# Padding a four-row broadcast matmul to 128 rows inside a fused attention and feed-forward kernel

## The chip, the cores and the metric

The kernel runs on one core of a Trainium2 chip. The metric is the device time of one execution in microseconds (us). Three runs of the kernel before gave 1332.72, 1333.96 and 1334.77 us, so the median is 1333.96 us. Engines are named TensorE (PE; PEld is its weight load), VectorE (DVE), ScalarE (ACT), GpSimd (POOL) and SyncE (SP, which here only issues DMAs).

## The reference

Three layers follow one another on a batch of 8 with 576 tokens: a linear attention with 8 heads of 64, a gated feed-forward (512 to 1024 and back), and a second one with a convolution over tokens.

```python
def phi(x):
    proj = np.einsum('bhsd,df->bhsf', x, w_phi)
    proj = proj - np.max(np.abs(proj), axis=-1, keepdims=True)
    return np.concatenate([np.exp(proj), np.exp(-proj)], axis=-1)
q_p, k_p = phi(q), phi(k)
kv = np.einsum('bhsf,bhsd->bhfd', k_p, v)
z = np.sum(k_p, axis=2)
num = np.einsum('bhsf,bhfd->bhsd', q_p, kv)
den = np.einsum('bhsf,bhf->bhs', q_p, z)[..., None] + 1e-06
x = num / den                                   # heads side by side: 512 wide
# first feed-forward: token shift, k = relu(xk @ w_k), v = k*k @ w_v
x = sigmoid(xr @ w_r) * v
# second: h = relu(x @ w_in), c = convolution of h over 3 tokens
out = (h * sigmoid(c)) @ w_out
```

## The kernel before

Heads go in pairs: 8 batches of 4 pairs, 32 pairs in all, and a pair makes one 128-row chunk of the transposed input of the first feed-forward. Attention of one pair runs beside the projections of the next one (function `attention`), and from pair 5 on the first feed-forward runs between attention's steps, a share at a time (`moe`). When attention ends, at about 830 us, the rest of the first feed-forward follows, then the second one. Most products are made of three products of halves in float32r ("hi" and "lo", `mm3`, L143 to L145).

The names in the trace: `ps` are projections (L247 to L251), `pkv` the products of keys and values (L304), `pt` transposes (L333), `pn` numerators with the denominator as 65th row (L359); `psk`, `psr`, `psv` belong to the first feed-forward, `psh` and `pso` to the second.

The division works like this. The two heads' denominators go by DMA into a tile `den` of 96 partitions; VectorE takes the reciprocal and splits it in hi and lo (`r4`); four DMAs on SyncE's queue (L386) lay these out as four rows of `rr`: two heads, hi and lo, 576 tokens each. Then the function `last` spreads each head's row over that head's 64 partitions with a matmul (L398): the stationary operand `on2` has 4 rows of ones and zeros and 128 columns, the moving one is `rr`, 4 rows and 288 columns, one half of the tokens at a time. The result `pr` is multiplied with the numerators into `xt` (L401), the chunk of the feed-forward's input. `last` is called a pair later, so that the DMAs have time.

There are 64 such matmuls, two for each pair. The order of the work is set by a scheduler that goes by its own costs, with attention's steps at higher priority than the feed-forward's; the two matmuls of a pair end up side by side or with other products between them.

```python
on2 = const.tile([4, P], F32R, name="on2")
V.tensor_copy(on2, on0)
...
rr = pool.tile([4, S], F32R, tag="rr", bufs=1, name="rr")
for i in range(4):
    SY.dma_start(f(rr[i:i + 1]), f(r4[:, i // 2, i % 2]))
...
T.matmul(pr, on2, rr[:, hf * HS:hf * HS + HS], start=True, stop=True)
```

Of the kernel before, what the change touches and what calls it, by code (L numbers as in the profile page):

```python
# [9 lines left out]
F32R = mybir.dt.float32r  # L10
# [5 lines left out]
P = 128  # L16
B, H, S, D = 8, 8, 576, 64
NP = H // 2          # head pairs; a pair is one 128-row chunk of d_model
DM, DFF, FT = 512, 1024, 128
KC = DM // P         # 4  # L20
FC = DFF // P        # 8
TMPS = 4             # tiles for what is soon used up
XT = 6               # chunks of x^T on chip
PSM = 3              # PSUM banks of the feed-forward while attention runs
# pairs from the first on whose projections and numerators take float32 products,
# while the tensor engine has time, and whose projections lie in the feed-forward's banks
NAT, NATN, PP = 6, 8, 5
# the feed-forward runs from the attention of pair MS on, slower up to pair SLOW
MS, SLOW, SR = 5, 9, 7.5
# steps of attention(pair) after which a part of the first feed-forward's weights is split  # L30
WAT = {p: (0, 8) for p in range(4)} | {-1: (0,), 4: (0, 4, 8, 12), 5: range(0, 17, 3), 6: range(17), 7: range(17)}
NB = 12              # the first of these parts, of 512 columns; the others have 256
DS0 = 10             # the second feed-forward's weights are split from this pair's attention on
HS = S // 2          # 288 tokens: one PSUM bank holds a half of a batch's tokens
V1 = D + 1
# columns of a head pair: q's tokens in order, k's last 64 tokens, k's first 512 tokens.
# Their nine tiles of 128 go by banks; the one in the middle holds the last 64 of q and of k.
W = 2 * S
BANKS = [(5, 6), (7, 8), (4,), (0, 1), (2, 3)]
DP = 6               # a head's 576 denominators as 96 partitions of 6  # L40


@with_exitstack
def fused_kernel(ctx: ExitStack, tc: tile.TileContext, qk, va, wphi, ones2, mu, wk, wv, wr, win, wout, cw, out):
# [9 lines left out]
    def f(x):  # L54
        return x.bitcast(F32)

    def from_f64(raw, h, c):
        """float32 of float64 given as their words, into c; h is room: cut to 24 bits,
        kept within float32's range, and zero below its normal numbers."""
        high, low = raw[:, :, 1], raw[:, :, 0]  # L60
        hu, cu = h.bitcast(U32), c.bitcast(U32)
        # the high word read as a float32 rises with the magnitude: 0x47efffff is that of the
        # largest float32; the squares of those of 2^-127 and 2^-126 lie around the threshold
        G.tensor_scalar(h, f(high), -122879.9921875, 122879.9921875, ALU.max, ALU.min)
        V.tensor_scalar(cu, hu, 3, 0x3FFFFFF8, ALU.logical_shift_left, ALU.bitwise_and)
        V.scalar_tensor_tensor(cu, hu, 0xC0000000, cu, ALU.bitwise_and, ALU.bitwise_or)
        V.scalar_tensor_tensor(cu, low, 29, cu, ALU.logical_shift_right, ALU.bitwise_or)
        A.activation(h, h, AF.Square)
        V.scalar_tensor_tensor(c, h, 2.0 ** -30 * 1.125, c, ALU.is_ge, ALU.mult)
# [14 lines left out]

# [1 line left out]
    ident = const.tile([P, P], F32, name="ident")  # L86
# [11 lines left out]
    V.tensor_tensor(wpl, wp0, f(wph), ALU.subtract)  # L98
    on2 = const.tile([4, P], F32R, name="on2")
    V.tensor_copy(on2, on0)  # L100
    mu1 = const.tile([P, 2, KC], F32, name="mu1")
    V.tensor_scalar(mu1, mu0, -1.0, 1.0, ALU.mult, ALU.add)
# [1 line left out]
    def weight(n, name):  # L104
        """Room for a weight [128, n], split."""
        hi = wpool.tile([P, 4096], F32R, tag="w", name=name + "h")
        lo = wpool.tile([P, 4096], F32R, tag="w", name=name + "l") if n == 4096 else None
        return hi[:, :n], lo[:, :n] if lo is not None else hi[:, n:2 * n]

    def weight_dram(src, name):  # L110
        """As above, into DRAM, by and by."""
        d = [dram.tile([P, 4096], F32, name=name + x) for x in "hl"]
        steps = []
        for o in range(0, 4096, 256):
            def load(o=o):
                raw = main.tile([P, 256, 2], U32, tag="raww", bufs=1, name="raww")
                SY.dma_start(raw, src[:, o:o + 256])
                return raw

            def step(raw, o=o):  # L120
                hc = tmps.tile([P, 2, 256], F32, tag="tmp", name="hc")
                from_f64(raw, hc[:, 0], hc[:, 1])
                w = tmps.tile([P, 2, 256], F32R, tag="tmp", name="whl")
                A.copy(w[:, 0], hc[:, 1])
                V.tensor_tensor(w[:, 1], hc[:, 1], f(w[:, 0]), ALU.subtract)
                for i in range(2):
                    SY.dma_start(d[i][:, o:o + 256], f(w[:, i]))
            steps.append((load, step))
        return d, steps
# [18 lines left out]

    # =============== attention and the first feed-forward ===============
    with ExitStack() as p1:  # L150
# [7 lines left out]
        def raw_room(n):  # L158
            # room that the feed-forward and the later pairs have no need of yet
            if n > 256:  # L160
                nraw[0] += 1
                return main.tile([P, 512, 2], U32, tag=("mh", "ml")[nraw[0] % 2], bufs=2, name="raw")
            nroom[0] += 1
            if nroom[0] % 3 == 2:
                return main.tile([P, 256, 2], U32, tag="raww", bufs=1, name="raw")
            return pool.tile([P, 256, 2], U32, tag="e", bufs=2, name="raw")

        def step(src, hs, ls, o, n):
            def run():
                w = early(src[:, o:o + n], n, raw_room(n))  # L170
                A.copy(hs[:, o:o + n], w)
                G.tensor_tensor(ls[:, o:o + n], w, f(hs[:, o:o + n]), ALU.subtract)
            return run

        wsteps = [step(wk, wkh, wkl, o, 512) for o in range(0, 4096, 512)]
        for h in range(2):
            for w in ((wr, wrh, wrl), (wv, wvh, wvl)):
                n = w[1].shape[1] // 2
# [14 lines left out]
        loaded, xk, xq, vts = {}, {}, {}, {}  # L193
        KC0 = 512  # the columns from here on are k's (and q's last 64)

        def load(Pi):
            """The columns of one of the first pairs: they take float32 products, with no split."""
            b, p = divmod(Pi, NP)
# [20 lines left out]
        def split(Pi, k):  # L219
            """Half of a pair's columns, split."""  # L220
            raw = loaded.pop((Pi, k))
# [13 lines left out]
        def project(Pi, js):  # L235
            """Projections [token, (head, feature)] less each token's maximum."""
            x = xk[Pi]
# [23 lines left out]
        def front_k(Pi):  # L261
# [9 lines left out]
            t = centred(*project(Pi, BANKS[2]), 1, "t1")  # L271
            # k's last 64 tokens, a head above the other
            k_ = pool.tile([P, 2, FT], F32, tag="kr", bufs=1, name="kr")
# [17 lines left out]
        def order(x):  # L291
            """TensorE keeps the order of these products: a long one hides the load of the next one's weights."""
            if chain:
# [3 lines left out]
        def sums(Pi):  # L297
            """Emitters of the products of kv and z."""
            kp, vt = kps_.pop(Pi), vts.pop(Pi)
# [19 lines left out]
        def queries(Pi, h):  # L319
            """Features of q, transposed."""  # L320
            t = ts[Pi]
# [28 lines left out]
        def numerators(Pi, h, other):  # L350
            """Numerators and denominators [dim, token]; between the products those of the next pair's kv."""
            kv, q_ = kvs[Pi], qs.pop(h)
# [22 lines left out]
        def finish(Pi):  # L375
# [7 lines left out]
            V.tensor_tensor(r4[:, :, 1], rd, f(r4[:, :, 0]), ALU.subtract)  # L383
            rr = pool.tile([4, S], F32R, tag="rr", bufs=1, name="rr")
            for i in range(4):
# [4 lines left out]
            def last():  # L390
                # x^T with a zero column in front
                while done[0] * NP <= Pi - XT:
# [22 lines left out]
        def attention(Pi):  # L415
            """The second half of pair Pi beside the first half of pair Pi + 1; Pi -1 has no second half."""
            nx, cur = Pi + 1 < B * NP, Pi >= 0
# [41 lines left out]
        def mix(u, j):  # L459
            """Time mix of half a batch, split: j 0 for k, 1 for r."""  # L460
            b, hf = divmod(u, 2)
# [81 lines left out]
        m = moe_all()  # L543
        # a share of the feed-forward behind each of attention's steps
        load(0)
# [26 lines left out]

    # =============== the end of it, and the second feed-forward ===============
    with ExitStack() as p2:
# [133 lines left out]
```

## Time and profile before

| | us |
|---|---|
| median of three runs | 1333.96 |
| the profiled execution, span of its instructions | 1332.9 |
| TensorE busy | 1315.1 (99%) |
| VectorE busy | 934.6 (70%) |
| ScalarE busy | 768.1 (58%) |
| GpSimd busy | 160.2 (12%) |

The profiled execution's own time is told as its span; the median of the runs is 1.06 us above it. Busy time of TensorE is modelled: products overlap, so a duration in a row (0.29 us for 288 columns) is longer than the step from one start to the next. PEclk is the clock that TensorE was granted, 1.00 being 2.4 GHz and 0.50 being 1.2 GHz.

### The profile page before, as it was taken

How to read it: one execution, taken by the hardware profiler on the slowest of the kernel's cores; microseconds unless marked ns; L12 is line 12 of the kernel's file. 1: busy time of each engine (PE TensorE's matmuls, PEld its weight loads, DVE VectorE, ACT ScalarE, POOL GpSimd, SP SyncE). 2: the span in 40 equal slices, each digit the busy share in tenths (PEclk: the TensorE clock that was granted, in tenths of full speed). 3: DMA queues.
4: the chain of work that ended last, by engine and by line, in shares of the span. 5: the costliest groups of instructions: out<-in, count | busy, mean ns of one | idle time of the engine just before them, and what ended most of it. 6: DMA issues, size and time to landing. Idle time of an engine off the chain costs nothing.

```text
span 1332.9 us, 25967 instructions
## 1 busy us (share of the span) xinstructions
PE 1315.1 (99%) x9962; PEld 1279.6 (96%) x9962; DVE 934.6 (70%) x1748; ACT 768.1 (58%) x1760; POOL 160.2 (12%) x250
## 2 busy tenths in 40 slices
PE   8889999999999999999999999999999999999998
PEld 6679999999999999999999999999999999999998
DVE  7979978789878878978976855442754744744743
ACT  5567766567666666565755644343654654654653
POOL 6534500111110111111100000000000000000000
PEclk9899999999999999999999999999999999999999
DMA  7313221322322322233211101305102102102110
GB/s 257 118 38 96 87 74 39 94 88 63 90 81 81 97 85 82 71 100 94 70 54 40 47 19 42 122 19 180 37 36 72 36 36 72 36 37 72 29 44 36
DMA packets 73932, 95.79 MB, mean 72 GB/s; under 512 B 26956, under 2 KB 51664, under 8 KB 73808
## 3 DMA queue, kind: packets, MB, share of 16 engines
q1 hardware_dynamic: 60016, 66.26, 15.6%
q0 software_dynamic: 4944, 18.29, 4.2%
q10 hardware_dynamic: 8848, 9.57, 2.5%
q8 instruction: 79, 1.29, 0.4%
q14 instruction: 45, 0.37, 0.1%
HBM read 66.39 MB, written 27.26 MB: 70 GB/s over the span
## 4 chain that ended last, share of the span: by engine, by line
PE 95%; DVE 3%; DMA 1%; issue 1%; ACT 0%; DVEq 0%; ACTq 0%
PE pn L359 8%; PE pkv L304 7%; PE psk L144 5%; PE psv L143 5%; PE psk L145 5%; PE psv L145 5%; PE psk L143 5%; PE psh L143 5%; PE psh L144 5%; PE psv L144 5%; PE pso L144 5%; PE pso L145 5%; PE psh L145 5%; PE pso L143 5%; PE psr L145 3%; PE psr L144 3%
## 5 line engine op out<-in xcount | busy, mean ns | idle before, releaser
L304 PEld LDWEIGHTS pkv<-va,kp 128*128 128x128 f32 x1024 | 156.6, 194 | 8.2 <-issue 1.2
L144 PE MATMUL psk<-ml,wkh 128*128 128x288 f32 x512 | 154.2, 301 | 1.3 <-DVE ml L471 1.3
L304 PE MATMUL pkv<-va,kp 128*128 128x65 f32 x1024 | 154.8, 255 | 0.0
L145 PE MATMUL psk<-mh,wkh 128*128 128x288 f32 x512 | 153.8, 300 | 0.0
L143 PE MATMUL psv<-kh,wvl 128*128 128x288 f32 x512 | 153.6, 301 | 0.0
L143 PE MATMUL psk<-mh,wkl 128*128 128x288 f32 x512 | 152.3, 299 | 0.2 <-ACT mh L470 0.2
L144 PE MATMUL psv<-kl,wvh 128*128 128x288 f32 x512 | 152.4, 298 | 0.0
L145 PE MATMUL psv<-kh,wvh 128*128 128x288 f32 x512 | 151.9, 297 | 0.0
L144 PE MATMUL psh<-xl,wih 128*128 128x288 f32 x512 | 151.1, 296 | 0.0
L143 PE MATMUL psh<-xh,wil 128*128 128x288 f32 x512 | 150.6, 296 | 0.0
L145 PE MATMUL psh<-xh,wih 128*128 128x288 f32 x512 | 150.1, 294 | 0.0
L144 PE MATMUL pso<-gl,woh 128*128 128x288 f32 x512 | 148.9, 295 | 0.0
L145 PE MATMUL pso<-gh,woh 128*128 128x288 f32 x512 | 148.7, 295 | 0.0
L143 PE MATMUL pso<-gh,wol 128*128 128x288 f32 x512 | 144.1, 293 | 0.0
L612 DVE SCALAR_TENSOR_TENSOR ct<-h,cw,ct 128x576 f32<-128x576 f32 x64 | 52.4, 818 | 102.6 <-ACT ct L611 102.3
L253 DVE TENSOR_REDUCE mx<-ps 128x4 f32<-128x512 f32 (+1 forms) x160 | 99.3, 625 | 23.2 <-PE ps L251 14.5
L504 ACT ACTIVATE kf<-psk 128x288 f32<-128x288 f32 x128 | 52.4, 410 | 84.9 <-PE psk L145 84.6
L144 PEld LDWEIGHTS psk<-ml,wkh 128*128 128x128 f32 x512 | 96.8, 189 | 4.5 <-DVE ml L471 1.8
L367 ACT COPY nd<-pn 65x288 f32<-65x288 f32 x128 | 49.7, 393 | 87.5 <-PE pn L359 78.3
L258 DVE TENSOR_TENSOR t<-ps,mx 128x512 f32<-128x512 f32 (+1 forms) x160 | 99.5, 627 | 0.8
L145 PEld LDWEIGHTS psk<-mh,wkh 128*128 128x128 f32 x512 | 97.1, 190 | 0.6 <-issue 0.2
L143 PEld LDWEIGHTS psv<-kh,wvl 128*128 128x128 f32 x512 | 96.3, 188 | 1.4
(122 smaller groups left out, 3793.3 us busy)
## 6 DMA issues: line engine op xcount, KB each, us to landing
va<-va SPq DMA_DIRECT2D x32, 325.0 KB, 3.2
x2s<-x SPq DMA_DIRECT2D x32, 288.0 KB, 2.5
x2r<-x2s ACTq DMA_DIRECT2D x32, 288.0 KB, 3.2
out<-ot SPq DMA_DIRECT2D x32, 288.0 KB, 2.1
rqk<-qk POOLq DMA_DIRECT2D x26, 320.0 KB, 3.1
rqk<-qk POOLq DMA_DIRECT2D x26, 256.0 KB, 2.9
raw<-wk SPq DMA_DIRECT2D x8, 512.0 KB, 5.6
raww<-win SPq DMA_DIRECT2D x16, 256.0 KB, 2.8
```

Of the source, the lines that this page charges most:

```text
L143: T.matmul(ps, wl, xh, start=first, stop=False)
L144: T.matmul(ps, wh, xl, start=False, stop=False)
L145: T.matmul(ps, wh, xh, start=False, stop=last)
L253: V.tensor_reduce(mx, ps, axis=AX.X, op=ALU.max, apply_absolute_value=True)
L258: V.tensor_tensor(t, ps, mx.unsqueeze(3).to_broadcast([P, n, 2, FT]), ALU.subtract)
L304: order(T.matmul(o, k_, v_, start=(i == 0), stop=(i == len(prods) - 1)))
L359: order(T.matmul(pn, kv[a][:, c, h], q_[i][:, c, w], start=(n == 0), stop=(n == len(prods) - 1)))
L367: A.copy(u[:, hf], pn)
L504: A.activation(kf[:, j], ps, AF.Relu)
L612: V.scalar_tensor_tensor(t, h[:, 1:S + 1], cw0[:, fc, 1:2], t, ALU.mult, ALU.add)
```

## The change

`on2` and `rr` become tiles of 128 partitions. Both are filled with zeros once by GpSimd; the four rows of ones are copied into the first four partitions of `on2`, and `rr` is made once, ahead of the loop, instead of anew for each pair. The four DMAs still write its first four rows, and the matmul takes all 128 rows of both; 124 of them are zero and add nothing. The comments are taken out as well, and the new lines shift the line numbers (L398 is L402 in the new kernel, the memsets are L101 and L178).

```diff
-    on2 = const.tile([4, P], F32R, name="on2")
-    V.tensor_copy(on2, on0)
+    on2 = const.tile([P, P], F32R, name="on2")
+    G.memset(f(on2), 0.0)
+    V.tensor_copy(on2[:4], on0)
...
+        rr = pool.tile([P, S], F32R, name="rr")
+        G.memset(f(rr), 0.0)
...
-            rr = pool.tile([4, S], F32R, tag="rr", bufs=1, name="rr")
             for i in range(4):
                 SY.dma_start(f(rr[i:i + 1]), f(r4[:, i // 2, i % 2]))
```

The scheduler orders the new program afresh. GpSimd's queue at the start, before:

```order
9 masks.py:197 MEMSET ident 128x128
10 L91 DMA on_76<-ones 4x128
11 L93 DMA mu_78<-mu 128x8
12 L204 DMA rqk<-qk 128x1152
13 masks.py:199 ISA
14 masks.py:199 AFFINE_SELECT ident<-ident 128x128
15 L64 TENSOR_SCALAR h<-raw 128x512 x2
```

And after:

```order
9 masks.py:197 MEMSET ident 128x128
10 L91 DMA on_76<-ones 4x128
11 L93 DMA mu_78<-mu 128x8
12 L101 MEMSET on_85 128x128
13 L178 MEMSET rr 128x576
14 L209 DMA rqk<-qk 128x1152
15 masks.py:199 ISA
16 masks.py:199 AFFINE_SELECT ident<-ident 128x128
17 L64 TENSOR_SCALAR h<-raw 128x512 x2
```

The two memsets stand ahead of the second load of queries and keys (`rqk`, pair 1) and of the end of the identity; nothing else moved here.

TensorE's queue where pair 0's transposes and pair 1's projections begin, before:

```order
7 L304 MATMUL pkv<-va,kr 128x130
8 L247 MATMUL ps<-wp_74,rqk 128x256 x4
9 L333 MATMUL pt<-ident,t 128x128
10 L247 MATMUL ps<-wp_74,rqk 128x256
11 L333 MATMUL pt<-ident,t 128x128 x2
12 L359 MATMUL pn<-qf,kvf 65x288 x3
```

And after:

```order
7 L309 MATMUL pkv<-va,kr 128x130
8 L338 MATMUL pt<-ident,t 128x128 x3
9 L252 MATMUL ps<-wp_74,rqk 128x256 x5
10 L364 MATMUL pn<-qf,kvf 65x288 x3
```

The same products stand here in another order; the other differences on TensorE are of this kind, and the last of them lies ahead of pair 3's `pr`.

TensorE's queue in the stage where attention and feed-forward run together (the place that ran at 228.6 to 230.5 us in the trace), before, with what each product waits for:

```order
999 L144 MATMUL psv<-kl,wvh 128x288
1000 L249 MATMUL ps<-wph,xl 128x256 [waits PE_49,Activation_49]
...
1005 L251 MATMUL ps<-wph,xh 128x256
1006 L398 MATMUL pr<-rr,on_85 128x288 [waits DMAHW2_49,DMAHW1_49,DMAHW3_49,DMAHW0_49,Activation_49]
1007 L398 MATMUL pr<-rr,on_85 128x288 [waits PE_49,Activation_49]
1008 L145 MATMUL psv<-kh,wvh 128x288
```

And after:

```order
1001 L146 MATMUL psv<-kl,wvh 128x288
1002 L254 MATMUL ps<-wph,xl 128x256 [waits PE_49,Activation_49]
...
1007 L256 MATMUL ps<-wph,xh 128x256
1008 L402 MATMUL pr<-rr,on_85 128x288 [waits DMAHW2_49,DMAHW1_49,DMAHW3_49,DMAHW0_49,Activation_49]
1009 L402 MATMUL pr<-rr,on_85 128x288 [waits PE_49,Activation_49]
1010 L147 MATMUL psv<-kh,wvh 128x288
```

Order and waits are the same here in both; the contracted rows (4 before, 128 after) are not shown in these rows.

## Rows read from the trace of the kernel before

**Rows 1.** The page: busy us (share of the span) xinstructions of each engine.
```profile
PE 1315.1 (99%) x9962; PEld 1279.6 (96%) x9962; DVE 934.6 (70%) x1748; ACT 768.1 (58%) x1760; POOL 160.2 (12%) x250
```

**Rows 2.** Busy time by stage; columns as the first line names them.
```profile
core 0: us, PE busy (x) PEld busy (x) DVE busy (x) ACT busy (x) POOL busy (x), PEclk, DMA share, GB/s
0.00:98.00 98.00, 83.82 (x448) 67.88 (x448) 81.69 (x155) 60.08 (x149) 50.88 (x48) 0.91 0.42 140
98.00:150.00 52.00, 51.86 (x378) 47.38 (x379) 49.04 (x109) 36.09 (x94) 24.97 (x26) 1.00 0.32 99
150.00:830.00 680.00, 680.00 (x5371) 665.08 (x5371) 550.79 (x1138) 418.16 (x1030) 78.06 (x114) 1.00 0.23 70
860.00:1333.00 473.00, 469.45 (x3543) 469.21 (x3542) 239.15 (x324) 241.45 (x461) 6.29 (x62) 1.00 0.16 53
```

**Rows 3.** TensorE's waits after 98 us: total us, times, longest.
```profile
PE pn L359 <- DVE t L258: 0.3, 1, 0.3
```

**Rows 4.** The tile `pr`: its matmuls in the trace, and its busy time by stage.
```profile
L398 PE MATMUL pr<-rr,on x64: 288/394/575, 42.2 to 827.5; 4*128 4x288 f32 x64
...
98.00:150.00 52.00, 1.57 (x4) 0.72 (x4) 5.40 (x12) 1.00 0.32 99
98.00:830.00 732.00, 20.23 (x56) 9.66 (x56) 52.30 (x116) 1.00 0.24 72
```

**Rows 5.** Timeline of PE around a single `pr`: start us, us, instruction.
```profile
116.10 0.29 PE L143 MATMUL psk<-mh,wkl 128*128 128x288 f32 x1
116.32 0.40 PE L398 MATMUL pr<-rr,on 4*128 4x288 f32 x1
116.64 0.40 PE L144 MATMUL psk<-ml,wkh 128*128 128x288 f32 x1
116.89 0.30 PE L145 MATMUL psk<-mh,wkh 128*128 128x288 f32 x1
117.02 0.29 PE L143 MATMUL psk<-mh,wkl 128*128 128x288 f32 x1
```

**Rows 6.** The same stretch, PEld (weight loads; in brackets idle time before).
```profile
116.32 0.18 PEld L398 LDWEIGHTS pr<-rr,on 4*128 4x128 f32 x1 [0.16 <-issue]
116.64 0.19 PEld L144 LDWEIGHTS psk<-ml,wkh 128*128 128x128 f32 x1
116.75 0.19 PEld L145 LDWEIGHTS psk<-mh,wkh 128*128 128x128 f32 x1
```

**Rows 7.** Timeline of PE around two `pr` side by side.
```profile
228.71 0.30 PE L144 MATMUL psv<-kl,wvh 128*128 128x288 f32 x1
228.84 0.28 PE L249 MATMUL ps<-wph,xl 128*128 128x256 f32 x1
...
229.20 0.28 PE L249 MATMUL ps<-wph,xl 128*128 128x256 f32 x1
...
229.43 0.28 PE L251 MATMUL ps<-wph,xh 128*128 128x256 f32 x1
229.64 0.53 PE L398 MATMUL pr<-rr,on 4*128 4x288 f32 x2
230.10 0.40 PE L145 MATMUL psv<-kh,wvh 128*128 128x288 f32 x1
230.34 0.30 PE L143 MATMUL psv<-kh,wvl 128*128 128x288 f32 x1
```

**Rows 8.** TensorE's waits over the span at `pr`.
```profile
PE pr L398 <- DMA rr<-r: 1.8, 1, 1.8
PE pr L398 <- ACT h L68: 1.5, 1, 1.5
PE pr L398 <- ACT nd L367: 0.9, 1, 0.9
```

**Rows 9.** Last pair: SyncE's issues, TensorE's timeline; then issues with median us to landing.
```profile
821.23 2.44 SPq L386 DMA_DIRECT2D rr<-r  x4
...
827.24 0.53 PE L398 MATMUL pr<-rr,on 4*128 4x288 f32 x2
...
rr<-r SPq DMA_DIRECT2D x128, 2.2 KB, 1.9
```

**Rows 10.** Timeline of GpSimd at the start.
```profile
2.15 0.22 POOL masks.py:197 MEMSET ident<- 128x128 f32 x1
...
3.39 0.53 POOL L204 DMA_DIRECT2D rqk<-qk  x1
...
8.19 1.95 POOL L64 TENSOR_SCALAR h<-raw 128x512 f32<-128x512 f32 x1 [3.87 <-DMA raw<-wk]
```

**Rows 11.** Busy time by stage, in one of three stretches at the lower clock.
```profile
44.30:51.10 6.80, 6.80 (x28) 5.72 (x27) 5.43 (x10) 2.72 (x6) 4.23 (x3) 0.50 0.47 162
```

## The prediction

> **What bounds the kernel now.** I read the page first, then the busy time by stage, then TensorE's waits, and only then single instructions. On the page TensorE is busy for 99% of the span, VectorE for 70%, the others less [rows 1]. A mean can hide a stage with another limit, so the stages come next. Up to 98 us TensorE is busy for 83.82 us; from 98 to 830 us it has practically no idle time, and VectorE, the next in line, is busy for 49.04 of 52 and then 550.79 of 680 us [rows 2]. TensorE's waits, which have nine entries over the whole span, hold a single one, of 0.3 us, after 98 us [rows 3]. So after 98 us the time is what TensorE's queue takes to run through its own instructions, and a change pays there only if it makes that queue shorter.
>
> Busy time cannot show whether it is as short as it could be, since modelled durations overlap: a product of 288 columns is given some 0.29 us, yet the next one starts 0.13 us later. The step from start to start is what counts. In the last stage 3543 products take 469.45 us [rows 2], 0.1325 us each; that is the price of a 288-column product in the stream.
>
> Now the matmul that the change touches, `pr`. It contracts 4 rows [rows 4] (the 4 ahead of the star), all others contract 128. Look at one that stands alone [rows 5]: 0.22 us pass from the start of the product before it to its own, 0.32 us to the next one, and 0.25 us more to the one after that; then the steps are 0.13 us again. From 116.10 to 116.89 us three steps take 0.79 us where three ordinary ones take 0.40, so this one costs 0.39 us above its own price. The weight loads show where it goes: ordinarily a load starts while the product before it runs (that of L145 at 116.75, under the product that began at 116.64), but `pr`'s load starts with its own product at 116.32, after 0.16 us in which the load path stood idle, and the load behind it starts with its product too, at 116.64 [rows 6]. The stream is broken on the way in and on the way out.
>
> Two `pr` side by side tell whether that is per matmul or per change of shape. From 229.43 to 230.34 us four steps take 0.91 us; one of a 256-column product (0.115 us, half of 229.20 to 229.43) and three of 0.1325 make 0.51 [rows 7]; both `pr` stand in one row there. The pair costs 0.40 us extra, no more than the single. So it is paid at each passage between 4 and 128 rows, about 0.195 us in and as much out.
>
> The Trainium skill says so outright (TensorEngine Tiling (Array Packing), Key Properties): a change of tiling mode, not of tile alone, drains the engine, and four contracted rows fall into its 32-row mode. The trace's 0.195 us for each passage agrees.
>
> **The change part by part.** *The 64 products.* With 128 rows on both sides `pr` has the shape of its neighbours, and there is no passage left. Its own price stays: 288 columns, 0.1325 us. I counted the groups in the order of TensorE's instructions: after 98 us there are 56 `pr` [rows 4], 42 alone and 7 pairs, so 49 groups at 0.39 us: 19.1 us. Ahead of 98 us are four pairs. Three of them come after a wait, for ScalarE or for the DMAs of `rr` itself [rows 8], which hides the way in; their way out (3 x 0.195) and the whole of the fourth (0.39) make 1.0 us at most, nothing at least, since that stage hangs on chains through other engines. I take the middle, 0.5.
>
> *Whether the saving stays.* TensorE is 19 us ahead at 830 us only if its feeders keep up. VectorE's 550.79 us from 150 to 830 would then fall into 662.5 us (45 groups, 17.5 us), 83% instead of 81%. It is fuller from 98 to 150 us, 94%, but only four groups lie there [rows 2, 4], 1.6 us. The products behind each `pr` are feed-forward work with its operands long made. The DMAs of `rr` are the nearest thing to being late: the last four are issued by 821.23 + 2.44 = 823.67 us and land 1.9 us later (median), 1.7 us ahead of `pr` at 827.24 [rows 9]. But that chain begins at TensorE's own numerators and moves up with it; only 0.39 us of the cover is at stake. I take nothing off, and 2 us as the bound: the four groups that lie where VectorE is fullest, and one more.
>
> *The memsets.* Two new instructions stand in GpSimd's queue, `on2` (128x128) and `rr` (128x576), ahead of a load's issue at 3.39 us and of the last step of the identity. The 128x128 memset of the identity took 0.22 us; 576 columns at that rate are 1.0 us; together 1.2 us. Behind them GpSimd idles for 3.87 us up to 8.19 us, waiting for a DMA [rows 10], so its own work is not late, and the load for pair 1 is issued at 4.6 us. Cost: 0, or 1.2 us if the cover fails.
>
> *The order.* `rr` is one tile instead of a new one per pair; each DMA into it still waits for the `pr` that read it last. The scheduler's order differs on all engines in the opening; on TensorE the last difference is at its 255th instruction, just ahead of the fourth pair's `pr` (97 us), and the 9015 behind it are the same. What this does to the first 98 us cannot be read off: 14.2 us of idle time lie there [rows 2], and three stretches, of 6.8, 6.9 and 3.4 us, in which the granted clock stood at 0.5, the lower level of 1.2 GHz [rows 11]. One such stretch more or less is 6.8 us at half speed, 3.4 us of time. I take 0 and keep 3.4 either way.
>
> Sum: 19.1 + 0.5 = 19.6 us off the profiled span of 1332.9, so 1313.3; the median of the runs lies 1.06 us above that span, so 1314.4 us.
>
> **The rivals.** *The load is still not taken ahead.* Suppose the padded load stays exposed, and only the rest of the break goes. A 128-row load takes 0.19 us [rows 6], 64 of them 12.2 us; the gain shrinks to 7.4 us: 1326.6. For it: `pr` is the one product whose load has a queue of waits ahead of it. Against: the 128-row loads beside it start ahead, and one that is not taken ahead would hold up a product that waits like it does, `ps` at 228.84, which is on time [rows 7]. The Trainium skill speaks for this rival (TensorE: Matmul & The Clock Gate, Part 3, The mechanism): loads overlap running products only where their row groups differ, which after padding they no longer do. The loads of L143 to L145 contradict it, all with 128 rows and all ahead.
>
> *The waits are the cost, not the shape.* `pr` waits for four DMAs, ScalarE and TensorE; these waits stay. Then nothing is gained: 1334. For it: the first `pr` of a pair always has them. Against: the `ps` at 228.84 us waits for the same TensorE and ScalarE semaphores as a second `pr`, and starts 0.13 us after its forerunner [rows 7]; and in the pair both members wait, yet the pair pays once.
>
> *Slower: the opening falls to the lower clock.* If the new order leaves TensorE idle longer ahead of 98 us, and the clock stands at 1.2 GHz for more of it, each us of full-clock work takes another. Of 83.8 us busy some 17 are at half already [rows 2, 11], so 67 are left to lose; the gain is gone once 19.6 of these run at half. With 25 of them it is 1339. For it: three such stretches occur already. Against: the reordering is of a few products among their likes, and no engine gains more than 1.2 us of work [rows 10].
>
> **How the numbers follow.** Forecast, all 49 breaks gone: 0.82, of which 0.08 with more than 3.4 us lost or won in the opening or to VectorE. Load exposed: 0.08. Waits: 0.06. Slower opening: 0.04. The forecast's own span is 1314.4 with 3.4 for the clock either way, 1311 to 1317.8; 2 us for late feeders and 1.2 for the memsets push the upper end to 1321, and half a us for the early groups the lower to 1310.5. Beyond that lie 0.18 for the rivals. About 0.2% (2.7 us) is what a measurement of this kernel can tell from no change: faster 0.90, within 0.06, slower 0.04.
>
> **What would show it.** In the profile after, `pr` should read 128 rows, take about 0.29 us like its neighbours, with its load ahead of it, and the steps around it should all be near 0.13 us; TensorE's time from the first `pr` after 98 us to the end of attention should be 19 us shorter, the last stage unchanged. Wrong would be: `pr` at 0.29 us with the steps still 0.22 and 0.32 (waits), a load starting with its own product (exposed load), new entries in TensorE's waits after 98 us (late feeders), or a longer opening with more half-clock time.

## The result and the profile after

The changed kernel takes 1319.44 us (median of four runs, 1317.54 to 1320.78), the kernel before 1333.64 (median of four, one run more than in the 1333.96 told ahead of the prediction); the ratio is 0.989, with a 95% interval of 0.9876 to 0.9904. That is 14.2 us less. The profiled execution has a span of 1319.0 us, 13.9 below the one before, where the forecast took off 19.6. The time lies within the range of 1310.5 to 1321, but above the 1311 to 1317.8 that the forecast gave before it added room for late feeders and for the memsets.

What the forecast said of `pr` itself came out as written. Tile `pr` in the trace of the changed kernel, weight loads and products (times in ns min/median/max, first and last start, rows contracted ahead of the star), answering [rows 4]:

```profile
L402 PEld LDWEIGHTS pr<-rr,on x64: 186/188/333, 45.7 to 813.6; 128*128 128x128 f32 x64
L402 PE MATMUL pr<-rr,on x64: 288/296/577, 45.7 to 813.7; 128*128 128x288 f32 x64
```

The single `pr` of [rows 5], now, on PE:

```profile
117.51 0.30 PE L145 MATMUL psk<-mh,wkl 128*128 128x288 f32 x1
117.65 0.29 PE L402 MATMUL pr<-rr,on 128*128 128x288 f32 x1
117.78 0.29 PE L146 MATMUL psk<-ml,wkh 128*128 128x288 f32 x1
117.91 0.30 PE L147 MATMUL psk<-mh,wkh 128*128 128x288 f32 x1
```

and its weight load, answering [rows 6]:

```profile
117.38 0.19 PEld L145 LDWEIGHTS psk<-mh,wkl 128*128 128x128 f32 x1
117.52 0.19 PEld L402 LDWEIGHTS pr<-rr,on 128*128 128x128 f32 x1
117.65 0.19 PEld L146 LDWEIGHTS psk<-ml,wkh 128*128 128x128 f32 x1
```

Three steps take 0.40 us (117.51 to 117.91) where they took 0.79, and `pr`'s load starts 0.13 us ahead of its product. The pair of [rows 7] passes at the ordinary pace too: 0.51 us from 228.97 to 229.48 instead of 0.91.

```profile
228.97 0.28 PE L256 MATMUL ps<-wph,xh 128*128 128x256 f32 x1
229.09 0.42 PE L402 MATMUL pr<-rr,on 128*128 128x288 f32 x2
229.35 0.29 PE L147 MATMUL psv<-kh,wvh 128*128 128x288 f32 x1
229.48 0.29 PE L145 MATMUL psv<-kh,wvl 128*128 128x288 f32 x1
```

Where, then, are the missing 5.7 us of span? Two marks cut the time in three: the start of the fourth pair's first `pr`, from which on TensorE's order is the same in both kernels, and the first product of the second feed-forward. The marks before:

```profile
97.33 0.53 PE L398 MATMUL pr<-rr,on 4*128 4x288 f32 x2
...
L143 PE MATMUL psh<-xh,wil x512: 289/295/299, 922.4 to 1303.5; 128*128 128x288 f32 x171
```

and after:

```profile
98.51 0.61 PE L402 MATMUL pr<-rr,on 128*128 128x288 f32 x2
...
L145 PE MATMUL psh<-xh,wil x512: 289/295/298, 908.5 to 1289.6; 128*128 128x288 f32 x171
```

The opening got 1.2 us longer (97.33 to 98.51); the stretch between the marks, where all 49 groups lie, fell from 825.1 to 810.0, by 15.1 instead of 19.1 us; the last stage is as long as it was, 410.5 us from its first product to the end of the span. So 1.7 us of the shortfall lie in the opening (a gain of 0.5 was forecast) and 4.0 behind it. By stage, answering [rows 2], and TensorE's waits behind 98.6 us, answering [rows 3]:

```profile
core 0: us, PE busy (x) PEld busy (x) DVE busy (x) ACT busy (x) POOL busy (x), PEclk, DMA share, GB/s
0.00:98.00 98.00, 80.45 (x443) 65.56 (x444) 80.14 (x152) 60.19 (x149) 51.59 (x50) 0.93 0.43 140
98.00:150.00 52.00, 50.86 (x375) 46.75 (x375) 48.84 (x107) 33.87 (x91) 24.31 (x25) 1.00 0.32 89
```

```profile
PE pn L364 <- DVE xT L405: 0.6, 1, 0.6
PE pn L364 <- DVE t L263: 0.5, 1, 0.5
PE ps L254 <- ACT kvf L313: 0.4, 1, 0.4
PE ps L254 <- DVE xl L234: 0.2, 1, 0.2
```

One wait of 0.3 us has become four, 1.7 us together; the prediction had named such new entries as a sign of late feeders. TensorE's idle time in the first 98 us grew from 14.2 to 17.6 us. Waits within the modelled duration of a product do not show in this list; they show when the two traces are laid beside each other product by product. The steps from the second product before each group of `pr` to the second one behind it are 19.0 us shorter in all 49 groups together, mostly 0.39 in each: the breaks gave back what they were priced at. All other steps are 3.6 us longer, and those at the fourth pair's own `pr` 0.3. TensorE loses 0.77 us at the `pn` of 143 us, 0.30 at 145.6, 0.65 at 151.5, and later 0.1 to 0.3 at a time, of it 0.9 from 556 to 567 us. The first of these waits for the VectorE step that reads `pr`; in the kernel before, the same `pn` started 0.13 us after its forerunner:

```profile
143.07 0.43 PE L364 MATMUL pn<-qf,kvf 128*65 128x288 f32 x1 [0.60 <-DVE xT L405]
```

### The profile page after: what moved, and what is told of

It reads as the page before. It is cut to its first block, busy times and chain, and to the rows that moved or that the text cites. A ratio compares the mean times of both kernels' runs of the same rounds, so it can differ in the third digit from the quotient of the medians.

```text
span 1319.0 us, 25962 instructions
## 1 busy us (share of the span) xinstructions
PE 1296.2 (98%) x9962; PEld 1274.0 (97%) x9962; DVE 932.2 (71%) x1748; ACT 765.6 (58%) x1760; POOL 155.8 (12%) x252
## 4 chain that ended last, share of the span: by engine, by line
PE 86%; DVE 6%; issue 2%; DMA 2%; ACT 2%; POOL 1%; SPq 0%; POOLq 0%; DVEq 0%; ACTq 0%
PE pn L364 6%; PE pkv L309 6%; PE psh L145 5%; PE psh L146 5%; PE pso L146 5%; PE pso L147 5%; PE psh L147 5%; PE pso L145 5%; PE psk L147 5%; PE psk L145 5%; PE psk L146 5%; PE psv L146 5%; PE psv L145 5%; PE psv L147 5%; PE psr L145 2%
## 5 line engine op out<-in xcount | busy, mean ns | idle before, releaser
L145 PEld LDWEIGHTS psk<-mh,wkl 128*128 128x128 f32 x512 | 96.3, 189 | 3.0 <-issue 2.4
L147 PEld LDWEIGHTS psv<-kh,wvh 128*128 128x128 f32 x512 | 96.4, 188 | 0.0
L146 PEld LDWEIGHTS psv<-kl,wvh 128*128 128x128 f32 x512 | 96.4, 188 | 0.0
```

The lines of the kernel that those rows point to most:

```text
L145: T.matmul(ps, wl, xh, start=first, stop=False)
L146: T.matmul(ps, wh, xl, start=False, stop=False)
L147: T.matmul(ps, wh, xh, start=False, stop=last)
```

## The experiments

**Shapes in a clean stream (e1_shapes).** The prediction read the price from a stage where products wait for one another. Here it is measured by itself, in the last stage, by one run of which only the trace is used. `SHAPES` holds the rows and output columns of each batch:

```diff
+                if c == 1 and SHAPES[b_[0]]:
+                    n, m = SHAPES[b_[0]]
+                    for i in range(1 + fc % 2):
+                        T.matmul(ps[1][:m], zz[:n, :m], xs_[1][0][:n, c], start=False, stop=False)
```

> The changed kernel with zero products added in the second feed-forward, where nothing but TensorE sets the time: in each of the 64 chunks one product (every second chunk: two side by side) of a zero operand is added into the running sum, so the result stays. They wait for nothing. Batch 0 has none, batch 1 has 4 contracted rows, then 32, 33, 64, 65 and 128 rows, and batch 7 has 128 rows with 32 output columns. Theory (array mode): the array is used in modes of 32, 64 and 128 rows, and each passage between modes costs 0.195 us; steps around the added product are 0.22, 0.32 and 0.25 us at 4 and 32 rows, broken by the same 0.39 us at 33 and 64, and 0.13 us at 65 and 128. A pair pays once. 32 columns are a mode of their own and cost 0.39 us too. Rival (few rows are slow as such): the extra shrinks with the rows, at 64 it is about half. Rival (waits): no extra anywhere, since these products wait for nothing; all steps 0.13 us.

With 64 rows the stream breaks (timeline of PE; the added product is `zz`):

```profile
1126.62 0.29 PE L150 MATMUL psh<-xh,wih 128*128 128x288 f32 x1
1126.84 0.40 PE L617 MATMUL psh<-xh,zz 64*128 64x288 f32 x1
1127.17 0.40 PE L148 MATMUL psh<-xh,wil 128*128 128x288 f32 x1
1127.41 0.29 PE L149 MATMUL psh<-xl,wih 128*128 128x288 f32 x1
```

With 65 it does not:

```profile
1182.13 0.30 PE L150 MATMUL psh<-xh,wih 128*128 128x288 f32 x1
1182.26 0.30 PE L617 MATMUL psh<-xh,zz 65*128 65x288 f32 x1
1182.40 0.29 PE L148 MATMUL psh<-xh,wil 128*128 128x288 f32 x1
1182.53 0.29 PE L149 MATMUL psh<-xl,wih 128*128 128x288 f32 x1
```

Nor with 128 rows and 32 output columns:

```profile
1286.96 0.29 PE L150 MATMUL psh<-xh,wih 128*128 128x288 f32 x1
1287.10 0.29 PE L617 MATMUL psh<-xh,zz 128*32 128x288 f32 x1
1287.23 0.29 PE L148 MATMUL psh<-xh,wil 128*128 128x288 f32 x1
1287.36 0.30 PE L149 MATMUL psh<-xl,wih 128*128 128x288 f32 x1
```

Over all places the extra is 0.39 us for a single at 4, 32, 33 and 64 rows, 0.39 for a pair, and 0.00 at 65 and 128. The products wait for nothing, so the waits are not the cost; 4 and 64 rows cost the same, so it is not fewness of rows. The 32 output columns were expected to break the stream and did not: that part of the theory is wrong.

**The change without its matmul (e2_memset_only).**

```diff
-                    T.matmul(pr, on2, rr[:, hf * HS:hf * HS + HS], start=True, stop=True)
+                    T.matmul(pr, on2[:4], rr[:4, hf * HS:hf * HS + HS], start=True, stop=True)
```

> The change without its matmul: both tiles have 128 rows and are zeroed, but the product takes the first four rows of each, as before. What it does to the opening and the scheduler's order is in, the padding is not. Theory (breaks at 49 groups are worth 19 us, and the changed opening and late feeders gave about 5 back, of it 1.7 in the opening): 1335.5 us, 1.7 above the kernel before, all of it ahead of 98 us. Rival (the opening costs all of what is missing): 1339. Rival (the gain came from the other order, not from the shape): 1319.

1336.28 us, a ratio of 1.0019 (1.0010 to 1.0028) to the 1333.53 of the kernel before, measured beside it: all that surrounds the padding costs 2.7 us. The fourth pair's `pr` starts at 98.94 us:

```profile
98.94 0.53 PE L402 MATMUL pr<-rr,on 4*128 4x288 f32 x2
...
L145 PE MATMUL psh<-xh,wil x512: 289/295/298, 925.1 to 1306.2; 128*128 128x288 f32 x171
```

So 1.6 us of it lie in the opening. The rest, 1.1 us, lies between the marks, mostly in steps at 150 to 162 us; nothing had been expected there. Between the marks it takes 826.2 us, and the padding takes that to 810.0, 16.2 less; in the runs it is worth 16.8 us (1336.28 to 1319.44). Ahead of the marks the two differ in more than the padding: TensorE's order is another one in 18 places. In the opening this run and the changed kernel lose the most at the same place, the first `pr`, which waits for the DMAs of `rr` (first this run, then the changed kernel):

```profile
45.73 0.81 PE L402 MATMUL pr<-rr,on 4*128 4x288 f32 x2 [3.89 <-DMA rr<-r]
```

```profile
45.73 0.82 PE L402 MATMUL pr<-rr,on 128*128 128x288 f32 x2 [3.95 <-DMA rr<-r]
```

In the kernel before it started at 42.18 us. The wait does not depend on the product's shape.

**64 and 65 rows in the kernel (e3_pad64, e4_pad65).** Both tiles with 64, or with 65 partitions:

```diff
-    on2 = const.tile([P, P], F32R, name="on2")
+    on2 = const.tile([64, P], F32R, name="on2")
-        rr = pool.tile([P, S], F32R, name="rr")
+        rr = pool.tile([64, S], F32R, name="rr")
```

> The change with 64 rows instead of 128 in both tiles. Theory (array mode of 64 rows, both passages stay): 1334 to 1336 us, steps around the product as before, 0.39 us of extra in each group. Rival (the extra goes down with the rows added): half the gain, 1327. Rival (any padding helps, as the load or the waits are what it mends): 1319.

> The change with 65 rows instead of 128 in both tiles, one more than the mode of 64 takes. Theory (array mode): the same as with 128 rows, 1319.4 us, steps of 0.13 us. Rival (only a full 128 rows let the load go ahead): 1334 to 1336. Rival (extra in proportion to missing rows): 1327.

64 rows: 1335.19 us, ratio 1.0013 (1.0004 to 1.0023); 65 rows: 1319.27 us, ratio 0.9886 (0.9869 to 0.9902). One row more is worth the whole gain, and these two kernels have the same order on every engine. `pr` and the marks, first with 64, then with 65 rows:

```profile
L402 PE MATMUL pr<-rr,on x64: 285/396/399, 46.0 to 827.4; 64*128 64x288 f32 x64
96.43 0.54 PE L402 MATMUL pr<-rr,on 64*128 64x288 f32 x2
...
L145 PE MATMUL psh<-xh,wil x512: 289/295/298, 922.3 to 1303.4; 128*128 128x288 f32 x171
```

```profile
L402 PE MATMUL pr<-rr,on x64: 289/298/485, 45.7 to 812.7; 65*128 65x288 f32 x64
97.56 0.64 PE L402 MATMUL pr<-rr,on 65*128 65x288 f32 x2
...
L145 PE MATMUL psh<-xh,wil x512: 289/295/298, 907.4 to 1288.6; 128*128 128x288 f32 x171
```

Between the marks that is 825.8 to 809.9 us, some 16.0 less. The kernel with 64 rows also has the order of e2_memset_only on every engine, and its `pr` breaks the stream as that one's does; yet its fourth pair's `pr` starts at 96.43 us, not 98.94. The first 98 us, first in e2_memset_only, then with 64 rows (columns as above):

```profile
0.00:98.00 98.00, 80.45 (x443) 65.84 (x444) 80.61 (x152) 59.85 (x147) 51.37 (x50) 0.93 0.43 140
0.00:98.00 98.00, 78.83 (x456) 63.39 (x457) 84.57 (x157) 60.54 (x149) 51.36 (x50) 0.98 0.43 140
```

So one and the same order gave openings 2.5 us apart in two executions, with a granted clock of 0.93 in one and 0.98 in the other. A difference of that size between the openings of two single traces, and the 1.2 and 1.6 us above are smaller, says little about the kernels by itself; the medians of the runs do.

**Another opening (e5_host_ones, e9_host_ones_4rows).** The ones come as 128 rows, `rr` is zeroed behind pair 1's load; the second run takes four rows of these tiles again.

```diff
-    on0 = tmps.tile([4, P], F32, tag="tmp", name="on0")
+    on0 = tmps.tile([P, P], F32, tag="tmp", name="on0")
-    G.memset(f(on2), 0.0)
-    V.tensor_copy(on2[:4], on0)
+    V.tensor_copy(on2, on0)
...
         load(1)
+        G.memset(f(rr), 0.0)
```

> The change with its constants brought in another way: the ones come as a 128-row array with zero rows, so `on2` needs no memset, and `rr` is zeroed by GpSimd behind the issue of pair 1's load instead of ahead of it. TensorE's order in the opening then differs from the kernel before in 8 places instead of 19 lines each way. Theory (what the opening cost, 2.7 us, comes from the order that the scheduler made of it): 1316.7 us, nearly 3 us faster than the change, with the fourth pair's `pr` back at 97 us. Rival (the order has no part in it, the opening swings by itself by 2 to 3 us from run to run): 1319.4.

> The faster version (ones brought as 128 rows, `rr` zeroed later) with its product cut back to the first four rows of both tiles; TensorE's order behind the fourth pair is the same. Theory (49 breaks are worth 16 to 17 us net on any opening, and the new opening alone is worth some 3 us against the kernel before): 1330 us, fourth pair's `pr` at 93 to 95 us, 16 to 17 above the version with 128 rows. Rival (the two help each other, the gain of the padding depends on the opening): 1325 or less, or 1334 with `pr` of the fourth pair back at 97.

e5_host_ones takes 1313.68 us, ratio 0.9851 (0.9836 to 0.9865): 5.8 us faster than the change, the fastest of all versions that compute the reference, and 3 us below the 1316.7 of its theory. Its fourth pair's `pr` starts at 93.59 us:

```profile
93.59 0.62 PE L400 MATMUL pr<-rr,on 128*128 128x288 f32 x2
...
L144 PE MATMUL psh<-xh,wil x512: 289/295/299, 902.6 to 1283.7; 128*128 128x288 f32 x171
```

With four rows it takes 1331.48, ratio 0.9985 (0.9971 to 0.9998): the new opening by itself is 2.4 us below the kernel before, barely clear of the noise (ten runs from 1328.87 to 1334.01). Its trace, of the slowest of these runs, has the fourth pair's `pr` at 96.19 us, where 93 to 95 were expected. The padding is worth 17.8 us on this opening in the runs, and 16.5 between the marks (825.5 to 809.0). So the gain of the padding hardly depends on the opening. The two ways of preparing the tiles differ by 4.8 us with four rows (1336.28 and 1331.48) and by 5.8 with 128. Whether the scheduler's order makes this, or the place and time of the memsets, is not shown: a run with no memset at all, in which DMAs bring the zero rows (e6_no_memset), gave no result.

**Is it VectorE's load? (e7_light_before, e8_light_after).** Both kernels with VectorE's last step of the weights' conversion left out:

```diff
-        V.scalar_tensor_tensor(c, h, 2.0 ** -30 * 1.125, c, ALU.is_ge, ALU.mult)
```

> The kernel before with less work on VectorE while weights are converted: the last step of the conversion (setting values below the normal numbers to zero) is left out, one instruction of about 0.65 us for 512 columns in each of the parts. Only a base for the next run. Theory: TensorE had no idle time behind 98 us, so little changes there; the opening may gain some us, as VectorE stands in its chain: 1325 to 1334. Rival (VectorE paces the whole of attention): 1320 or less.

> The changed kernel with the same step of the weights' conversion left out. Theory (of the 19.1 us that the breaks were worth, some 2.5 went to TensorE waiting for VectorE and ScalarE in places, above all from 140 to 160 us): with the feeders lighter the waits go and the difference from the fourth pair's `pr` to the second feed-forward grows from 16.2 to 18 to 19 us, the total to 17 to 19 below the run before it. Rival (the missing part is not VectorE's: the breaks hid something else, or cost less than 0.39 us each in a crowded stream): still 16 us.

1328.74 and 1316.06 us, 12.7 apart; between the marks 825.2 and 811.1, 14.1 apart. The scheduler made 47 groups here, so 18.3 us were due and 4.2 are missing. The theory that one step less on VectorE would bring the missing part back is refuted. Five waits are listed, 2.3 us together; the longest now is for a step of the reciprocals (the two longest behind 98 us, e8_light_after):

```profile
PE pn L363 <- DVE r L386: 1.0, 1, 1.0
PE ps L253 <- ACT kvf L312: 0.5, 1, 0.5
```

**Or the whole conversion? (e10_copy_before, e11_copy_after).** One VectorE copy in place of GpSimd's clamp, ScalarE's square and VectorE's four steps:

```diff
-        G.tensor_scalar(h, f(high), -122879.9921875, 122879.9921875, ALU.max, ALU.min)
...
-        V.scalar_tensor_tensor(c, h, 2.0 ** -30 * 1.125, c, ALU.is_ge, ALU.mult)
+        V.tensor_copy(c, f(high))
```

> The kernel before with the conversion of the weights from float64 left out: a single VectorE copy of the high words stands in its place, so GpSimd's clamp, ScalarE's square and three of VectorE's four steps go (the weights' values are not the right ones). Base for the next run. Theory: the opening gets shorter by 10 us or more, since its chains run through these steps; behind the fourth pair TensorE's time stays at 825 us.

> The changed kernel with the same conversion left out. Theory (what is missing of 19.1 us behind the fourth pair goes to waits for VectorE's queue, held up by the conversion's chain over GpSimd, ScalarE and VectorE): without the chain the difference between the two from the fourth pair's `pr` to the second feed-forward is 18.5 to 19.5 us, with no waits of 0.3 us or more between 130 and 180 us. Rival (the waits come from attention's own chains, or the breaks are worth less than 0.39 us): 15 to 16.5 us as before.

1321.93 and 1306.82 us, 15.1 apart; both compute with wrong weights. Between the marks, first e10_copy_before, then e11_copy_after:

```profile
86.11 0.53 PE L390 MATMUL pr<-rr,on 4*128 4x288 f32 x2
...
L135 PE MATMUL psh<-xh,wil x512: 289/295/298, 909.6 to 1290.7; 128*128 128x288 f32 x171
```

```profile
87.53 0.61 PE L394 MATMUL pr<-rr,on 128*128 128x288 f32 x2
...
L137 PE MATMUL psh<-xh,wil x512: 289/295/298, 894.1 to 1275.3; 128*128 128x288 f32 x171
```

823.5 to 806.6 us, 16.9 less. In these two the scheduler made 46 groups of the 56 `pr`, so 46 x 0.39 = 17.9 us were due, and a single wait is left that accounts for the difference (e11_copy_after):

```profile
PE pn L356 <- ACT qf L336: 1.0, 1, 1.0
```

So without the conversion all the small waits but one are gone, and each break yields its 0.39 us. The expected 18.5 to 19.5 was missed, since it supposed 49 groups and no wait at all. VectorE's busy time from 98 to 150 us fell from 48.84 to 38.14 here, and to 46.68 with the one step left out:

```profile
98.00:150.00 52.00, 50.98 (x382) 47.39 (x381) 38.14 (x84) 37.83 (x99) 14.10 (x22) 1.00 0.35 99
```

## Why the prediction was right, and where it was off

*The breaks (49 x 0.39 us).* Right, to the hundredth: 0.39 us per group in a clean stream, paid once for neighbours, gone with 65 rows or more. The 19.1 us did come free at `pr`, 19.0 by the steps around it. Only this sum is measured. That it is 0.195 on the way in and as much out is not shown: of the extra with 64 rows in e1, 0.09 us lie ahead of the start of the product and 0.30 behind it.

*"I take nothing off, and 2 us as the bound."* This is the step that failed. The stretch between the marks gained 4.0 us less than the 19.1 of the breaks. In it e2 is 1.1 us longer than the kernel before already, with four rows; against e2 the padding gave 16.2, so 2.9 us, more than the bound, were lost again as TensorE came earlier (3.1 between 64 and 65 rows). The argument was that feeders with 81 to 94% load keep up on average. An average does not tell when the one step that a product waits for is done: where VectorE is 94% busy (98 to 150 us), `pn` at 143 us waited for one VectorE step, and TensorE coming 0.39 us earlier per group then only waited longer. The place was named and its price was set at the four groups that lie there and one more, but the losses ran on, to 152 us and in small waits up to 567 us. That the conversion of the weights stands behind most of it is shown by e10 and e11, where 1.0 us is missing; which of its steps on which engine, is not: one VectorE step less was not enough.

*The opening (0 taken, 3.4 either way).* What surrounds the padding cost 2.7 us in e2, of it the 1.1 us behind the opening that are counted above; with 64 rows and the same order it was 1.7 us (1333.53 to 1335.19). The 3.4 us are about the size by which one order swings from execution to execution (2.5 us). The memsets' own time (0 or 1.2 us) was not separated from the order. What e5 and e9 show is that another way of preparing the same tiles takes some 5 us less. The profile pointed at the place (three waits of `pr` [rows 8]); the sign could not be read from it.

*The early groups (0.5 gained).* Not shown. Against the kernel before, the steps at the fourth pair's `pr` got 0.3 us longer, and the openings of single traces swing by more than the term.

*Where the order stops differing.* The prediction has this at TensorE's 255th instruction, with 9015 behind it. In the traces it is the 436th product of 9962, with 9526 behind it; what was concluded from it, the same order from the fourth pair on, holds.

*The range.* The mechanism of the gain was right; that the time fell into the range is in part luck. The range had room above for the clock, for late feeders and for the memsets. Two losses came, a slower opening without a lower clock and late feeders above their bound, and together they fitted into that room.

*The rivals.* The exposed load fell with the load at 117.52 us, 0.13 ahead of its product. The waits fell with e1, whose products have none, and with the step from 64 to 65 rows, which leaves all waits of `pr` in place. The slower opening was there in kind, with idle time (17.6 us instead of 14.2) rather than the lower clock (0.93 granted instead of 0.91), and in size far below the 19.6 us at which it decides.

The rule that spoke against the change, of the Trainium skill (TensorE: Matmul & The Clock Gate, Part 3, The mechanism), is that loads overlap running products only where row groups differ; the same section adds, as another case, a load into the background weight buffer. The "only" is contradicted by these runs: padded to 128 rows, `pr`'s load starts at 117.52 us, while the product of 117.51 runs. Whether the other case explains it, no run here shows. The Trainium skill says that a change of tiling mode drains the engine (TensorEngine Tiling (Array Packing), Key Properties); the 0.39 us there and back at 64 rows or fewer agree. The Trainium skill lists 128 rows by 32 columns as a mode of its own (same page, Tiling Modes); 32 output columns at 128 rows cost nothing in e1, and whether that product ran in such a mode is not shown.

## What to carry to other kernels

In this stream of 128-row products, a lone product with 4 to 64 rows cost three extra steps (0.39 us, where a step is 0.13), and the trace shows it only in the steps from start to start around it and in a weight load that does not run ahead. Pad such a product with zeros past 64 rows (65 did as well as 128), or put two side by side, since a pair paid once. When the bound engine gets faster, look for the stretch in which the next engine is fullest: here it was 94% busy, and the gain was not kept in full, however good the average. And where a scheduler orders the program, try two ways of preparing the same data, since two ways differed here by some 5 us, a third of the gain, for a reason that stays open.

## What was not expected of the hardware

The price did not depend on how few rows the product has: 0.39 us there and back at 4, 32, 33 and 64 rows alike, and nothing at 65. And a product with 32 output columns between products with 128 cost no more than its own 0.13 us.
